# Cross-shaped window attention: where the last stores are issued, how the last sums are grouped, when the second queries are projected, and the order of the work

## The chip, the cores and the metric

The kernel runs on one core of one Trainium2 chip. The metric is the device time of one execution in microseconds. A core has five engines that run side by side, each with its own list of instructions: TensorE (PE, with its weight loads shown apart as PEld), VectorE (DVE), ScalarE (ACT), GpSimd (POOL) and SyncE (SP). They wait for each other only through semaphores. DMAs are issued from the queue of an engine: here SP issues nearly all, ScalarE a few at the beginning and the end.

## The reference

The input x is an image of 224 x 224 positions with 96 channels, in bf16. It is projected to queries, keys and values of 96 channels each. The first 48 channels attend within horizontal stripes of 8 rows, the other 48 within vertical stripes of 8 columns; there are 28 stripes of each kind, and each has 1792 positions. The two halves of the result are put side by side and projected once more.

```python
qkv = jnp.einsum('bhwc,cd->bhwd', x, wqkv)
...
ah = _softmax(jnp.einsum('bqc,bkc->bqk', qh, kh) * scale, axis=-1)
oh = jnp.einsum('bqk,bkc->bqc', ah, vh).reshape(B, H, W, C2)
...
av = _softmax(jnp.einsum('bqc,bkc->bqk', qv, kv) * scale, axis=-1)
ov = jnp.einsum('bqk,bkc->bqc', av, vv).reshape(B, nw, H, sw, C2)
...
return jnp.einsum('bhwc,cd->bhwd', o, wo)
```

## The kernel before, in words

**Pairs, chunks and units.** Two stripes are worked on at once, as a pair P: pairs 0 to 13 are horizontal, 14 to 27 vertical. The 1792 queries of a pair are cut into four chunks (512, 512, 512 and 256, the list CH), the 1792 keys into 14 tiles of 128. A unit is the scores of one key tile (two for the small chunk) against one chunk, for both stripes: 128 x 1024 numbers in two banks of PSUM. TensorE makes them at L1015.

**Two ways to the exponential.** Most units, 1071 of them, go to ScalarE, which takes the exponential from PSUM into a buffer PT (L1037). The others, 301, go to VectorE, which builds the exponential out of integer operations: L1075 turns the scores into integers I_sb, L1088 and L1090 split off two parts (U_sb, E_sb), and L1094 multiplies (G_sb), partly on VectorE and partly on GpSimd in halves of 512. The values are then summed with these weights by TensorE at L968, into one bank a chunk. The 1 that is put beside the values gives the sum of the weights as well.

**What goes on around it.** For each pair the queries (L686, evacuated at L700), keys (L686, L706, centred at L720) and values (L761, L766) are projected while the pair before is worked on. Each finished chunk is copied out of PSUM (L931) and projected with wo: for horizontal pairs at L809, divided by the sum of the weights and kept in Ph_sb (L796, L816); for vertical pairs at L843 (or L847), divided into tmp (L796, L853), added to Ph_sb by GpSimd (L859) and stored (L887).

**The head.** Pair 0 has no pair before it. TensorE makes warm-up matmuls (L532), turns one half of x (L647), projects the keys and the first queries, and two groups of values (L761). Then come the second queries (one matmul at L686, two at L679), then the first scores (L1015). The keys are centred on VectorE in two pieces (L719), the first of 256 columns so that the first scores can start.

**The tail.** In the last pair stores go out in pieces of 16 x 8 x 96, one for each key tile's worth of queries and stripe. Those of the first two chunks, and those of the third chunk's first stripe, are issued by SP (L887); the four of the third chunk's second stripe by ScalarE, behind its last exponential. For the last, small chunk there is no addition on GpSimd: VectorE takes a reciprocal and makes four sums (L866, one a piece of 128 x 96, each a multiply by the reciprocal and an addition of Ph_sb), and four final stores follow (L898), two from SP and two from ScalarE. At the end SP waits until all stores have landed.

**What sets the order.** All instructions are made as records (Op) with the engine, the records they depend on and the buffers that they take. Each engine has several streams of such records: on TensorE 0 is the start-up, 1 and 2 are scores for ScalarE and VectorE, 3 and 4 the value sums of VectorE's and ScalarE's units, 5 output projections, 6 projections of the next pair. Strings of digits in PLAN say, for TensorE, VectorE and GpSimd, from which stream the next instruction comes; "bank" says which PSUM bank each takes and "far" which half products go to GpSimd. The order of each engine is thus written out, and each instruction waits for the semaphores of what it depends on. SP and ScalarE take what is ready by the planner's own reckoning of times.

Of the kernel before, what the change touches and what calls it, by code (L numbers as in the profile page):

```python
# [28 lines left out]
def ndc(P, c):  # L29
# [5 lines left out]
        "00000000000000000066611216162164144116444216331216431241641231431643441163446141541234133164412164412144312314"  # L35
        "31631451431244144126143153121433146124153341143444131235144123414414126413311463643164154134143163124614412614"
        "31145444134124163135164123135412144414412433112344144116344416312351431241641134445312416411463344144121543123"
        "14611364451231441163441233154113444412614412416312513411433444146123153114634413351541241634124136144123144116"
        "34434134124136134125144412316411463441213341146354154164144123133412314412414412316341163444135123164135414124"
        "41441461231634124133113644413312541441231641146344124313411634312441341261441231341441233144114644512316433153"  # L40
        "12416412314313411644431154444416415431531361241544123164114634114453341541231641241634125144144124133114434412"
        "54144113336412461441164431245143126134114533441414612351331241641146343124414411363412531441134464126134125144"
        "12413313412341541441163533416124415312461341144431163444412134412416313361441241541241631146441132331544113444"
        "12641441261331231341145444415412316311463433125144123164114534412341641146334144125413413312416441241641136441"
        "12444133113644312416441215431341241344123144164133123161331146345124153411444412361341134444615415416431313512"
        "44164123164114344412316311453441264134125144144124313312514414414611363354131254144123413416412416411463343141"
        "45124416313412416341241461113443344125144412133316412164412415411433334154124146134126133411634412441544121633"
        "11433544144164123154123146311446341241441164333125144113644512314314412441441612313412361341153444126133411263"
        "41441153444123416411463431333124154124163411264414411534441163354123164145123134412144414613312414312316441231"
        "44146135135312414414412613331163441144464451441331631241534124164114634114433441251344114644126314412514414123"  # L50
        "13412315411344436131641253144124163413514412416411463334143123146124134114644441214461133344125143411442154136"
        "12316412313313414412415441136446133125413124415411364441231544114634413313316441261341241641231441641144334125"
        "41341441231341241541241641146333134415413124414126133123154113644412315441146334154164144412613312316312464144"
        "11644341241334114634124415412415313613412413314364411444412531213314412313414313441241541163344143123154123154"
        "41146346114644611444463134151244415412316412416314412416411333441251344141153344412513341441241341241543164133"
        "14416412316312461441146443123144116336415312415314124413416412416412416412313313415441146341253134123154114464"
        "31244136144115343341431631241631241644126134114644412413311464441231334151244154124164124133113464431152344131"
        "34125134414412313415411463344154164164123163312416313464144126144144123153312414414412315312416411463331344164"
        "31441246144125144313412414414414615312361331231541136444412415411464441133644311344431531241531241641231641146"
        "44412413314441251334141125313341123444136144125144411463331463134125144412416411444334121641163363151244154124"  # L60
        "16312414316412164411433431231541144434415123315441231541144344123416411463341441246144121633113343412416441116"
        "36336124154124153124164134146124133124134134144415412415311633631541264431441254144134114334413441261331446121"
        "63414441231441126413311463441241541241531231614612431431331444144125143123314414412315441115336346113444641541"
        "64146163313613412414412614411344441231534124154124164114644412313412133411464441133633124415412315411344431251"
        "44411433441541241421316311366334166144164123134124144124154123153411466441313412441441231334154124153114444451"
        "312351331144444123313411434412541331241544113444124314311443152334154114421433114431433151534414445"),
    "dve": (
        "00000000000000000333333332332344323232443233313443432323244123443234323321342444133234423233333344133232333414"
        "23334323442322144313233244333233441323323333244312344323232344431323343133332342432344143232332344123443333332"
        "42421234413332344342333232144323323443214442323442424133321333244233344333331333233234431333323234243324124331"  # L70
        "32344323323344133323323444231323443323233244412334333132332443332144323233234431234432323244431333234312332344"
        "33233314423323234432144323423432412443123333244332344333333313323234412333234432321443233133323443232333413342"
        "32324431423443232324443134332312344323323344331323323443231233344234423321234431323234434323344132332323443313"
        "33234423442332124423133334423233443333132332344312333234421233244331332334432332334413232443231234432333234442"
        "41233431323323344323344413332323244314234423233234441344423132323344323344333313232323443214432332333444423144"
        "21244442343233441323323333334431333233234423231442313334234423233441343232334442133333423443232323444123343123"
        "32334443234441333323232344321444323323323214434441323234443233443331333234233442312344232332344344132314234442"
        "33332332334132334344441333233232344321444213323444323233443132332344432133333233244323234441233441332332344432"
        "34413232344432313332332334423324444412332313333323442344413423332444213234432332332334444421214423323333344333"
        "33333132234412332332344421234443132332344323441334232343333343242123323344334424412332313443432334442414423323"  # L80
        "34442144332343424444143333133333"),
    "pool": (
        "00000000022222221212122222222222222222112122222222222222221212122222222222222222221112222222222222222222211122"
        "22222222222222222121212222222222222222221212122222222222222222212112222222222222222222221212122222222222222222"
        "21212122222222222222222221112222222222222222222121212222222222222222222121212222222222222222222212121222222222"
        "22222222212121222222223223222232222121213222233332222322222121212222233322332232222333112122222222233223322331"
        "21213222232222332222121213222222333223222221211322222222333322222213131322223332222322222233321212123223222233"
        "2222222121212332232222223333221311222222332222222222212121232233332232222222222313112233322223333322333333"),
    "far": (
        "11111011110111111101111111111111111011111111110111011111111111111111101111111111111111111111111101111111111111"  # L90
        "11110111111111111111110111111111111111111111111110111011101100111111110010010111111010101101111001110111010111"
        "011110101100110110110111101101110111011100101101111111101011111011010100001000000"),
    "bank": (
        "76547012376502064256045260426402640264026046207420742047024702470240642053053205203520346034604163416416431463"
        "12356135375073057305730460247024602460406240640635046240260426013601376024072407240720420742706420462042604620"
        "43026402640261356035063503603650361356135631573173510357124571351753153153023520375137512642651365135713602460"
# [281 lines left out]
def bass_standalone__window_attn_cswin__vision_kernel(  # L378
# [30 lines left out]
    with es:  # L409
# [780 lines left out]
        def _(e):  # L1190
            emit(e, "sp")
            for b in range(2):
                n = pl.dma_tot.get(id(s_out[b]), 0)
                if n:
                    e.wait_ge(s_out[b], n)
# [28 lines left out]
```

## Time and profile before

| | us |
|---|---|
| median of three runs | 1008.08 |
| the three runs | 1008.08, 1011.19, 1004.94 |
| the profiled execution | 1004.3 |
| its span, first to last instruction | 1002.5 |
| TensorE busy | 988.0 |
| ScalarE busy | 987.6 |
| VectorE busy | 938.5 |
| GpSimd busy | 684.2 |

The profile is of one execution. A line such as L1037 is a line of the kernel before. In a group of instructions "x1071" is their count, and the numbers behind the bar are busy time in us, mean length of one in ns, and idle time of the engine just before them with what ended it. In the timeline the first two columns are start and length in us; instructions of a kind that follow each other are drawn together. "SPq" and "ACTq" are the instructions by which an engine issues a DMA. The granted clock of TensorE is 0.999 of full speed over the execution.

### The profile page before, as it was taken

What the parts mean: (1) busy time and instruction counts of PE and PEld (TensorE: products, weight loads), DVE (VectorE), ACT (ScalarE), POOL (GpSimd) and SP (SyncE); (2) the same over time, 40 slices, a digit from 0 to 9 for tenths busy, and PEclk for the clock granted to TensorE, in tenths of its full rate; (3) what the DMA queues carried; (4) which work ended last, traced back from release to release, by engine and by line L of the source; (5) the groups of instructions that cost most, each with busy time, mean ns of one, the idle gap of its engine ahead of it and who ended that gap; (6) DMA issues with size and microseconds to landing.
All of it is one profiled execution on the core that took longest, in us unless ns stands there. A gap on an engine that the chain in (4) does not pass through costs nothing.

```text
span 1002.5 us, 24560 instructions
## 1 busy us (share of the span) xinstructions
PE 988.0 (99%) x10211; PEld 385.9 (38%) x10211; DVE 938.5 (94%) x1573; ACT 987.6 (99%) x1080; POOL 684.2 (68%) x660
## 2 busy tenths in 40 slices
PE   8999999999999999999999999999999999999997
PEld 3433433343343334334334333433433443343342
DVE  8999999999999999999899999999999999999997
ACT  7999999999999999999999999999999999999997
POOL 3676766667677676777776776776676777677652
PEclk9999999999999999999999999999999999999999
DMA  5102120220112023011111122222122221222012
GB/s 110 39 2 38 38 32 8 38 38 1 39 39 32 8 38 38 2 36 25 27 29 32 25 46 50 54 52 44 34 41 52 53 54 39 52 52 40 13 36 50
DMA packets 164712, 36.92 MB, mean 37 GB/s; under 512 B 164488, under 2 KB 164488, under 8 KB 164600
## 3 DMA queue, kind: packets, MB, share of 16 engines
q1 hardware_dynamic: 163016, 34.80, 18.5%
q8 instruction: 80, 1.31, 0.5%
q10 hardware_dynamic: 1584, 0.55, 0.2%
q14 instruction: 32, 0.26, 0.1%
HBM read 0.44 MB, written 9.63 MB: 10 GB/s over the span
## 4 chain that ended last, share of the span: by engine, by line
ACT 70%; PE 29%; DVE 1%; issue 0%
ACT PT L1037 70%; PE ps L968 13%; PE ps L1015 11%; PE ps L686 2%; PE ps L761 1%; PE ps L843 1%; PE ps L532 0%; PE ps L809 0%; DVE OT_sb L931 0%; PE ps L647 0%; DVE out_sb L866 0%; DVE I_sb L1075 0%; DVE E_sb L1090 0%; DVE U_sb L1088 0%; PE ps L679 0%
## 5 line engine op out<-in xcount | busy, mean ns | idle before, releaser
L1037 ACT ACTIVATE PT<-ps 128x1024 bf16<-128x1024 f32 x1071 | 983.5, 1119 | 2.9 <-PE ps L1015 1.5
L1094 POOL TENSOR_TENSOR G_sb<-I_sb,U_sb 128x512 bf16<-128x512 bf16 x482 | 544.0, 1153 | 250.7 <-DVE E_sb L1090 225.3
L1015 PE MATMUL ps<-QT_sb,KT_sb 48*128 48x512 bf16 (+1 forms) x3136 | 463.0, 356 | 4.7 <-ACT PT L1037 3.0
L1075 DVE TENSOR_SCALAR I_sb<-ps 128x1024 int16<-128x1024 f32 x301 | 367.3, 1220 | 24.6 <-PE ps L1015 21.1
L968 PE MATMUL ps<-PT,V_sb 128*64 128x512 bf16 (+1 forms) x2422 | 363.8, 363 | 1.1 <-ACT PT L1037 1.0
L1015 PEld LDWEIGHTS ps<-QT_sb,KT_sb 48*128 48x128 bf16 x3136 | 123.2, 93 | 307.4 <-ACT PT L1037 223.7
L968 PEld LDWEIGHTS ps<-PT,V_sb 128*64 128x64 bf16 x2422 | 119.2, 109 | 122.5 <-issue 94.9
L968 PE MATMUL ps<-G_sb,V_sb 128*64 128x512 bf16 (+1 forms) x714 | 115.6, 356 | 0.0
L968 PE MATMUL ps<-E_sb,V_sb 128*64 128x512 bf16 (+1 forms) x714 | 109.9, 356 | 0.6 <-DVE OT_sb L931 0.2
L1088 DVE TENSOR_SCALAR U_sb<-I_sb 128x2048 int16<-128x2048 int16 (+1 forms) x161 | 109.2, 678 | 0.2
L859 POOL TENSOR_TENSOR out_sb<-tmp,Ph_sb 128x480 bf16<-128x480 f32 (+1 forms) x84 | 84.9, 1026 | 30.0 <-DVE E_sb L1090 10.7
L1090 DVE TENSOR_SCALAR E_sb<-I_sb 128x2048 int16<-128x2048 int16 (+1 forms) x161 | 104.9, 652 | 0.2 <-PE ps L968 0.2
L686 PE MATMUL ps<-xT_sb,w_sb 96*64 96x512 bf16 (+1 forms) x444 | 77.6, 367 | 0.9 <-ACT PT L1037 0.5
L931 DVE CAST OT_sb<-ps 128x512 bf16<-128x512 f32 x112 | 69.3, 619 | 5.9 <-PE ps L968 5.0
L706 DVE TENSOR_SCALAR_CACHE_REDUCE KT_sb<-ps 128x512 bf16<-128x512 f32 x110 | 67.8, 620 | 7.4 <-PE ps L686 6.8
L700 DVE TENSOR_SCALAR QT_sb<-ps 128x512 bf16<-128x512 f32 (+1 forms) x111 | 68.1, 619 | 5.2 <-PE ps L686 4.1
L766 DVE CAST V_sb<-ps 128x480 bf16<-128x480 f32 (+2 forms) x85 | 51.7, 611 | 3.1 <-PE ps L761 2.8
L968 PEld LDWEIGHTS ps<-G_sb,V_sb 128*64 128x64 bf16 x714 | 36.4, 108 | 47.3 <-issue 28.8
L720 POOL TENSOR_SCALAR KT_sb<-KT_sb,negmean 128x1792 bf16<-128x1792 bf16 x27 | 47.5, 1759 | 10.3 <-DVE E_sb L1090 6.2
L816 DVE TENSOR_TENSOR Ph_sb<-ps,rc 128x480 bf16<-128x480 f32 (+1 forms) x84 | 52.2, 622 | 2.1
L853 DVE TENSOR_TENSOR tmp<-ps,rc 128x480 f32<-128x480 f32 (+1 forms) x84 | 51.9, 618 | 2.2
L968 PEld LDWEIGHTS ps<-E_sb,V_sb 128*64 128x64 bf16 x714 | 33.9, 108 | 43.1 <-issue 21.1
(47 smaller groups left out, 324.4 us busy)
## 6 DMA issues: line engine op xcount, KB each, us to landing
out_dram<-out_sb SPq DMA_DIRECT2D x208, 42.0 KB, 2.1
xT_sb<-in_x_dram SPq DMA_TRANSPOSE x251, 2.4
out_dram<-out_sb SPq DMA_DIRECT2D x22, 24.0 KB, 1.9
Ph_sb<-in_x_dram ACTq DMA_DIRECT2D x1, 336.0 KB, 3.0
out_dram<-out_sb ACTq DMA_DIRECT2D x6, 24.0 KB, 1.9
wo_sb<-in_wo_dram SPq DMA_DIRECT2D x4, 9.0 KB
wo_sb<-one_sb SPq DMA_DIRECT2D x4, 0.0 KB
w_sb<-in_wqkv_dram ACTq DMA_DIRECT2D x1, 54.0 KB, 4.6
```

The lines of the kernel that those rows point to most:

```text
L686: ins = e.matmul(bk[64 * w:64 * w + 64, 0:qs], lhsT=w_sb[0:C, wblk(P, kind), :], rhs=rhs, start=True, stop=True)
L700: return e.tensor_scalar(dst, src, QS, None, ALU.mult)
L706: return e.tensor_scalar(dst, src, 1.0, None, ALU.mult, ALU.add, accum_out=acc)
L859: return e.tensor_tensor(out_sb[b][:, k0:k0 + nk, ws[0], :], t, Ph_sb[:, k0:k0 + nk, j0 + ws[0], :], ALU.add)
L931: return e.tensor_copy(OT_sb[b][:, q0:q0 + qs], bk[:, 0:qs])
L968: return e.matmul(bank(k.bank)[64 * w:64 * w + 64, x0:x1], lhsT=lhs(w, kts[i])[p0:p1], rhs=rhs(w, i, qs)[p0:p1, x0:x1], start=(op.tok["fir ...
L1015: ins = e.matmul(bank(op.tok["s"][w])[:, i * qs:(i + 1) * qs], lhsT=KT_sb[b][64 * w:64 * w + C2, kt * 128:(kt + 1) * 128], rhs=QT_sb[b][64 ...
L1037: a.fn = lambda e: e.activation(PT[a.tok["p"]][:].rearrange("p (s n) -> p s n", s=2), two(q.tok["s"]), ACTF.Exp, scale=LN128)
L1075: return e.tensor_scalar(dst[:, at:at + 1024].rearrange("p (s n) -> p s n", s=2), two(src), 128.0 * ONE, 0.0, ALU.add, ALU.max)
L1088: f.fn = lambda e: e.tensor_scalar(U_sb[y()][:, 0:m], I_sb[y()][:, 0:m], M_FRAC, HALF, ALU.bitwise_and, ALU.bitwise_or)
L1090: x2.fn = lambda e: e.tensor_scalar(E_sb[x2.tok["l"]][:, 0:m], I_sb[y()][:, 0:m], M_EXP, E_LOW, ALU.bitwise_and, ALU.bitwise_or)
L1094: g.fn = lambda e: e.tensor_tensor(G_sb[x2.tok["l"]][:, i0:i1], I_sb[y()][:, i0:i1].bitcast(BF16), U_sb[y()][:, i0:i1].bitcast(BF16), ALU. ...
```

## The change

There are four parts.

1. The four stores of the third chunk's first stripe in the last pair go from SP's queue to GpSimd's, behind the additions there, with a semaphore of their own (s_tail) for which SP waits at the very end.
2. The four last sums become two planned operations of two sums each. Within an operation the two instructions follow without a wait, one signal is given behind both, and then two stores are put out, one from SP and one from ScalarE.
3. The projection of the second queries of pair 0 is held back until the first scores have been issued.
4. All strings of PLAN are new: the order of instructions on TensorE, VectorE and GpSimd, the banks, and the half products that go to GpSimd.

The numbers of units on each engine are as before. The diff without the strings:

```diff
-        s_nat = sem("s_nat")
+        s_nat, s_tail = sem("s_nat"), sem("s_tail")
...
                 if kind == "q":
                     q_ready[(P, c)] = ops[0]
+                    if startup and c == 1:
+                        q_next.append(p)
...
-                    def d4(s, hold=hold, ws=ws, nk=nk, k0=k0):
+                    def d4(h, hold=hold, ws=ws, nk=nk, k0=k0):
                         def f(e, bk, op):
-                            w, k = ws[s // nk], k0 + s % nk
-                            return e.scalar_tensor_tensor(out_sb[b][:, k, w, :], bk[:, s * (C + 1):s * (C + 1) + C], rc[hold[0].tok["r"]][:, s:s + 1],
-                                                          Ph_sb[:, k, j0 + w, :], ALU.mult, ALU.add)
+                            for s in (h, h + 1):
+                                w, k = ws[s // nk], k0 + s % nk
+                                ins = e.scalar_tensor_tensor(out_sb[b][:, k, w, :], bk[:, s * (C + 1):s * (C + 1) + C], rc[hold[0].tok["r"]][:, s:s + 1],
+                                                             Ph_sb[:, k, j0 + w, :], ALU.mult, ALU.add)
+                            return ins
                         return f
...
-                            side = "act" if P == NP - 1 and c == NCH - 2 and ws[0] else "sp"
-                            dm = Op(side, 0.64, 2.0, fn, by + ([act_of[-1]] if side == "act" else []), dma=(s_out[b], 0))
-                            (q_first["act"] if side == "act" else sp_out).append(dm)
+                            side = ("act" if ws[0] else "pool") if P == NP - 1 and c == NCH - 2 else "sp"
+                            dm = Op(side, 1.0 if side == "pool" else 0.64, 2.0, fn, by + ([act_of[-1]] if side == "act" else []), dma=(s_tail if side == "pool" else s_out[b], 0))
+                            (q_first["act"] if side == "act" else pool_o if side == "pool" else sp_out).append(dm)
...
-                            if s == n - 1:
+                            for s in (h, h + 1):
+                                w, k = ws[s // nk], k0 + s % nk
+                                dst = bass.AP(out.tensor, out.offset + (16 * k * W + SW * (j0 + w)) * C, [[W * C, 16], [1, SW * C]])
+                                side = "act" if s % 2 else "sp"
+                                dm = Op(side, 0.64, 2.0, lambda e, dst=dst, k=k, w=w: e.dma_start(dst, out_sb[b][:, k, w, :]), [op], dma=(s_out[b], 0))
+                                (q_first["act"] if side == "act" else sp_out).append(dm)
+                            if h:
                                 rcs.free(hold[0].tok["r"], [op])
...
-                    tail = [("dve", 0.25, d4(i), [], True, dve_ev, [], final(i)) for i in range(n)] if last else [
+                    tail = [("dve", 0.54, d4(i), [], True, dve_ev, [], final(i)) for i in (0, 2)] if last else [
...
             q.kind = "qa"
+            if i == 0:
+                q_next[0].soft = list(q_next[0].soft) + [q]
...
+            n = pl.dma_tot.get(id(s_tail), 0)
+            if n:
+                e.wait_ge(s_tail, n)
```

The numbers in Op are the planner's own costs of an instruction; they steer where SP and ScalarE place an instruction and are no measurements. In the kernel after, the lines below the first change have numbers that are one to eleven higher.

More of the change, by code (lines that the diff above doesn't have):

```diff
@@ new lines @@
+    "pool": (
+        "00000000022222121212222222222222222222121212222222222222222222121122222222222222222221212122222222222222222211"
+        "21222222222222222222221212122222222222222222212121222222222222222221212122222222222222222222121212222222222222"
+        "22222121212222222222222222212121222222222222222222121212222222222222222222221212122222222222222222121212222222"
+        "22222222222221212122222222332222222232233121212222332232233222231311222222223223333322121212222322222222223221"
+        "31313223222232233322222121313222222223333222222121212222333222233222233131212223222232222222221213132222223333"
+        "22332222313112222322223223222233121212222223222233222231313122332222322322222213131322322322223333322332233333"
+        "33"),
```

149 lines of the change are left out of this document (69 added, 80 removed).

## The prediction

> **What bounds the kernel now.** I read the busy shares of the page first, then the chain that ended last, then the waits of ScalarE, the pace of its exponentials stage by stage, and last the two ends of the span.
>
> ```profile
> span 1002.5 us, 24560 instructions
> ...
> PE 988.0 (99%) x10211; PEld 385.9 (38%) x10211; DVE 938.5 (94%) x1573; ACT 987.6 (99%) x1080; POOL 684.2 (68%) x660
> ...
> ACT 70%; PE 29%; DVE 1%; issue 0%
> ...
> L1037 ACT ACTIVATE PT<-ps 128x1024 bf16<-128x1024 f32 x1071 | 983.5, 1119 | 2.9 <-PE ps L1015 1.5
> ```
>
> The reader should see that two engines are named 99% busy, and that the chain puts 70% on ScalarE. One line, the exponential L1037, holds ScalarE for 983.5 of 1002.5 us. TensorE's 99% is softer, as the waits tell:
>
> ```profile
> PEld ps L1015 <- ACT PT L1037: 223.7, 696, 0.8
> ...
> ACT PT L1037 <- PE ps L1015: 1.5, 3, 0.7
> ACT PT L1037 <- PE ps L968: 0.9, 4, 0.3
> ```
>
> TensorE's weight loads for the scores wait 223.7 us for ScalarE to give back banks; ScalarE stands visibly idle for 1.5 + 0.9 = 2.4 us. So the span is three pieces: a head until the first exponential, 1071 exponentials in a row, and a tail behind the last. The middle is paced like this (source view of L1037 in windows; the last two times of a row are the starts of its first and last exponential):
>
> ```profile
> L1037 ACT ACTIVATE PT<-ps x1071: 1018/1116/1300, 9.9 to 994.4; 128x1024 bf16<-128x1024 f32 x179
> ...
> L1037 ACT ACTIVATE PT<-ps x98: 1018/1085/1236, 9.9 to 99.7; 128x1024 bf16<-128x1024 f32 x98
> ...
> L1037 ACT ACTIVATE PT<-ps x111: 1029/1112/1300, 299.0 to 399.8; 128x1024 bf16<-128x1024 f32 x111
> ...
> L1037 ACT ACTIVATE PT<-ps x109: 1018/1109/1257, 699.6 to 799.5; 128x1024 bf16<-128x1024 f32 x109
> ...
> L1037 ACT ACTIVATE PT<-ps x105: 1041/1163/1278, 899.2 to 994.4; 128x1024 bf16<-128x1024 f32 x105
> ```
>
> One exponential lasts 1.1 us but overlaps the next, so the pace is the distance of starts: 984.5/1070 = 0.9201 us in all, 89.8/97 = 0.9258 in the first window, 100.8/110 = 0.9164, 99.9/108 = 0.9250, and 95.2/104 = 0.9154 in the last. The best and the worst window are 1.1% apart: there is waiting in the pace that the idle column, which counts only what the overlap doesn't cover, leaves out.
>
> **Part 1: four stores from SP's queue to GpSimd's, last sums in two operations.** The tail of before, from the timeline:
>
> ```profile
> 993.70 1.78 POOL L859 TENSOR_TENSOR out_sb<-tmp,Ph_sb 128x384 bf16<-128x384 f32 x2 [4.12 <-DVE tmp L853]
> ...
> 994.39 1.21 ACT L1037 ACTIVATE PT<-ps 128x1024 bf16<-128x1024 f32 x1
> ...
> 995.66 0.41 PE L968 MATMUL ps<-PT,V_sb 128*64 128x256 bf16 x4 [0.51 <-ACT PT L1037]
> ...
> 996.11 0.42 DVE L931 CAST OT_sb<-ps 128x256 bf16<-128x256 f32 x1 [1.80 <-PE ps L968]
> ...
> 996.99 0.18 DVE L796 RECIPROCAL rc<-ps 128x4 f32<-128x4 f32 x1 [0.46 <-PE ps L847]
> 997.21 1.38 DVE L866 SCALAR_TENSOR_TENSOR out_sb<-ps,rc,Ph_sb 128x96 bf16<-128x96 f32 x4
> ...
> 989.76 9.67 SPq L887 DMA_DIRECT2D out_dram<-out_sb  x13
> ...
> 995.69 2.80 ACTq L887 DMA_DIRECT2D out_dram<-out_sb  x4
> 998.54 1.26 ACTq L898 DMA_DIRECT2D out_dram<-out_sb  x2
> 999.48 1.26 SPq L898 DMA_DIRECT2D out_dram<-out_sb  x2
> ```
>
> The last sums (L866) are over at 997.21 + 1.38 = 998.59, but SP still works off older stores without a pause: thirteen from 989.76 to 999.43. Its two final stores (L898) go out only at 999.48 and 1000.1. What one costs:
>
> ```profile
> L898 SPq DMA_DIRECT2D out_dram<-out_sb x2: 597/606/615, 999.5 to 1000.1; - x2
> ...
> DMA to landing us min/median/max: 1.9/1.9/1.9
> ...
> SPq L1195 <- DMA out_dram<-out_sb: 1.3, 1, 1.3
> ```
>
> So the last store starts at 1000.1 and lands 1.9 later, at 1002.0; SP waits 1.3 us for it, and the span ends 0.5 later. Four stores fewer leave SP some 4 x 0.65 = 2.6 us earlier, near 996.8, ahead of the first sum: SP then issues when the sums are ready, its last near 998.6, landing at 1000.5. Next in line is ScalarE's queue, which the change leaves as it is: four stores from 995.69, two more at 998.54, the last starting at 998.54 + 0.65 = 999.2 and landing at 1001.1. That is 0.9 us before 1002.0, and I take this as the gain of the tail. If ScalarE's four stores also go at 0.65 (2.6 instead of 2.80 us) it is 1.1.
>
> The four stores on GpSimd stand behind the two additions L859, which end at 993.70 + 1.78 = 995.48; nothing but the end of the program is queued behind them, and SP waits for their own semaphore last of all. The trace of before has no DMA issue on GpSimd, so I bound it. From below: an issue on SP, 0.65 us; the fourth starts at 995.48 + 3 x 0.65 = 997.4 and lands, with 1.9, at 999.3. From above, the longest instruction that GpSimd has at all:
>
> ```profile
> L720 POOL TENSOR_SCALAR KT_sb<-KT_sb,negmean x27: 1758/1758/1761, 31.1 to 948.2; 128x1792 bf16<-128x1792 bf16 x27
> ```
>
> At 1.76 us the fourth starts at 1000.8 and lands at 1002.7. I take 0.9, GpSimd's own smaller step just before (1.78/2): 998.2 and 1000.1, hidden behind ScalarE's 1001.1. The ends make +0.7 of the tail (1002.7 against 1002.0) in place of -0.9.
>
> [...]
>
> The sums in two operations: two instead of four rounds of issue and signal. VectorE operations that don't wait for each other overlap:
>
> ```profile
> 975.09 0.68 DVE L1088 TENSOR_SCALAR U_sb<-I_sb 128x2048 int16<-128x2048 int16 x1
> ...
> 975.69 0.69 DVE L1090 TENSOR_SCALAR E_sb<-I_sb 128x2048 int16<-128x2048 int16 x1
> ```
>
> Starts 0.60 apart at 0.68 long: 0.08 of overlap, against 1.38/4 = 0.345 apart now. Two pairs save at most 2 x 0.12 = 0.24 us, and the first store waits up to 0.3 longer for its pair. Both lie under ScalarE's queue, which is busy until 998.5: cost and gain 0. If that cover went (stores off ScalarE too), the 0.24 would show.
>
> **Part 2: second queries projected behind the first scores.**
>
> ```profile
> 8.88 0.38 PE L686 MATMUL ps<-xT_sb,w_sb 96*64 96x512 bf16 x1
> 8.91 0.60 PE L679 MATMUL ps<-xT_sb,w_sb 96*64 96x256 bf16 x2
> 9.04 0.94 DVE L719 TENSOR_SCALAR KT_sb<-KT_sb,negmean 128x256 bf16<-128x256 bf16 x2
> 9.43 0.11 PEld L1015 LDWEIGHTS ps<-QT_sb,KT_sb 48*128 48x128 bf16 x4 [0.41 <-DVE KT_sb L719]
> ...
> 9.87 13.10 ACT L1037 ACTIVATE PT<-ps 128x1024 bf16<-128x1024 f32 x14 [0.71 <-PE ps L1015]
> 9.90 1.22 DVE L766 CAST V_sb<-ps 128x480 bf16<-128x480 f32 x2
> ...
> 11.03 0.68 DVE L700 TENSOR_SCALAR QT_sb<-ps 128x512 bf16<-128x512 f32 x1
> ...
> 11.63 1.22 DVE L1075 TENSOR_SCALAR I_sb<-ps 128x1024 int16<-128x1024 f32 x1
> ```
>
> Three matmuls leave the place ahead of the first scores. But the scores' weight load at 9.43 waits for the keys on VectorE (L719), not for them; only the end of the projection, 8.91 + 0.60 = 9.51, overhangs 9.43, by 0.08. The gain at the first exponential is between 0 and 0.1; I take 0.1. The moved evacuation (L700, 0.68 us) leaves its place ahead of VectorE's first own exponential, which may start up to 11.63 - 11.12 = 0.5 earlier, behind the value copies. The second queries serve the second chunk, and the first has ten units for ScalarE, some 9 us: the projection has cover. What VectorE gains here is not on the chain (DVE 1%): 0.
>
> **Part 3: the order searched anew.** By the instruction lists the two kernels have the same matmuls and the same 1071 exponentials; two half products move from VectorE to GpSimd. So only the pace can change. Bounds from the windows: 1070 x 0.9154 = 979.5, which is 5.0 less than 984.5; 1070 x 0.9258 = 990.6, 6.1 more. No row says which stalls the new order makes or ends: I take 0, the middle of the two but for 0.5 us, and keep both ends.
>
> **Sum.** -0.9 - 0.1 + 0 = -1.0 us. Against the profiled execution, 1004.3 us (span 1002.5 and 1.8 around it), 1003.3. That execution is the fastest of the four known: 1004.3, 1004.94, 1008.08, 1011.19. The middle of the four is (1004.94 + 1008.08)/2 = 1006.5, and I put the sum there: 1005.5 us, since a median is wanted, and no row explains why others took longer.
>
> **Rivals.** First, the new order is better: all stages at the best window's pace, -5.0, that is 1000.5 us. For it: the spread of windows, and 223.7 us in which TensorE waits and could work ahead. Against it: the visible idle of ScalarE is only 2.4 us.
>
> Second, the other side: the new order is worse. With every bank and buffer bound to an order written out, one late product makes TensorE, and so ScalarE, wait; at the first window's pace everywhere it is +6.1, 1011.6 us. It makes the kernel slower from a pace of 0.9201 + 1.0/1070 = 0.9211 on. For it: half of the quoted windows run slower than that already.
>
> Third, GpSimd's stores land last. It begins at 1.24 us an issue (995.48 + 3 x 1.24 + 1.9 = 1001.1) and eats the tail's whole gain at 1.54. At 1.76, +0.7 - 0.1: 1007.1 us. [...]
>
> Fourth, the tail's stores were not what ended it: then the last landing stays at 1002.0 though SP is idle before, and the time is 1006.5 - 0.1 = 1006.4.
>
> **How the numbers follow.** Forecast (pace within 2 us of before, tail 0.9 shorter) 0.45, with an own range of 1003.3 to 1007.1, the sum on the fastest execution and on the median of the runs; better order 0.25; worse order 0.18; GpSimd last 0.09; tail unchanged 0.03. The range takes in forecast, GpSimd, the unchanged tail and most of the two orders: 1000.5 to 1011.0, which leaves out a third to a half of each order's chance, some 0.18. About 1% is what a measurement of this kernel can tell from no change. Faster than 998.0 needs 2.5 us beyond the best pace: a fifth of the better order, 0.05. Slower than 1018.2 needs 6.6 beyond the worst: a fifth of the worse order, 0.04. Within 1%: 0.91.
>
> **What would show it.** In the profile after, SP's last small stores should end near 997, its final two start near 998 to 999, and the last landing be one of ScalarE's queue, 5.5 to 6 us behind the last exponential's end; a GpSimd issue over 1.24 us, or SP waiting longest for the new semaphore, speaks for the third rival. The first exponential should start 0 to 0.1 earlier, VectorE's first I_sb up to 0.5. The distance from the first to the last exponential, over 1070, is the whole verdict on the order: under 0.918 the first rival, over 0.922 the second. Wrong altogether would be a pace change over 1%, or a tail longer than before.

## The result, and the profile after

| | median us | range us | executions |
|---|---|---|---|
| before | 1006.16 | 1003.33 to 1012.10 | 20 |
| after | 1013.38 | 1008.70 to 1019.46 | 20 |

The ratio is 1.0061 [1.0045, 1.0077] (95% interval): the change makes the kernel 0.6% slower. Single executions of either kernel differ by up to 1.1%, and the longer ones have the lower mean granted clock (after: 1008.70 us at 0.997, 1019.46 at 0.989; before: 1002.92 at 0.998 and 1012.42 at 0.990 among the 23 beside e10); the profile of after (1014.82 us, clock 0.992) is close to its median, that of before (1004.3 us, 0.999) is among the fastest.

The page of after: the span, the chain that ended last by engine, and the exponential's group.

```profile
span 1012.9 us, 24541 instructions
...
ACT 63%; PE 32%; SPq 3%; DVE 1%; issue 1%; DMA 0%; DVEq 0%
...
L1045 ACT ACTIVATE PT<-ps 128x1024 bf16<-128x1024 f32 x1071 | 985.3, 1115 | 12.3 <-PE ps L1021 11.1
```

The exponentials are as long as before (1115 ns against 1119), and there are 1071 of them again. What has grown is the idle time of ScalarE in front of them, from 2.9 to 12.3 us; and SP's queue, which had no share in the chain before, has 3%. The exponentials start between 9.7 and 1005.4 in place of 9.9 and 994.4:

| piece of the span | before | after | difference |
|---|---|---|---|
| head, to the first exponential | 9.87 | 9.67 | -0.20 |
| first to last exponential | 984.53 | 995.71 | +11.18 |
| last exponential's start to the end | 8.10 | 7.56 | -0.54 |
| span | 1002.5 | 1012.9 | +10.4 |

So the tail is shorter, as forecast, and the middle eats it twenty times over. These are two single profiles, 10.4 us apart; the medians are 7.2 apart. The waits of TensorE name the place: here the longest wait of its matmuls in after, then TensorE, ScalarE and SP around it (timeline), and the same stretch in windows. A window's row gives its length, busy time and count for PE, PEld, DVE, ACT and POOL, then the granted clock, the DMA share and GB/s.

```profile
PE ps L687 <- issue: 2.9, 1, 2.9
```

```profile
599.13 11.01 SPq L892 DMA_DIRECT2D out_dram<-out_sb  x16
610.18 18.31 SPq L559 DMA_TRANSPOSE xT_sb<-in_x_dram  x14
628.54 11.42 SPq L892 DMA_DIRECT2D out_dram<-out_sb  x16
```

```profile
L559 SPq DMA_TRANSPOSE xT_sb<-in_x_dram x7: 1240/1241/1926, 640.0 to 648.4; - x7
...
DMA to landing us min/median/max: 2.4/2.5/4.0
```

```profile
647.61 0.41 PE L974 MATMUL ps<-PT,V_sb 128*64 128x256 bf16 x4
650.88 0.41 PE L687 MATMUL ps<-xT_sb,w_sb 96*64 96x512 bf16 x2 [2.86 <-issue]
...
651.62 0.64 PE L974 MATMUL ps<-PT,V_sb 128*64 128x256 bf16 x4
```

```profile
643.01 5.88 ACT L1045 ACTIVATE PT<-ps 128x1024 bf16<-128x1024 f32 x6
651.73 1.02 ACT L1045 ACTIVATE PT<-ps 128x1024 bf16<-128x1024 f32 x1 [2.84 <-PE ps L1021]
653.27 1.94 ACT L1045 ACTIVATE PT<-ps 128x1024 bf16<-128x1024 f32 x2 [0.52 <-PE ps L1021]
656.50 1.02 ACT L1045 ACTIVATE PT<-ps 128x1024 bf16<-128x1024 f32 x1 [1.29 <-PE ps L1021]
```

```profile
650.88:651.40 0.52, 0.52 (x4) 0.21 (x4) 0.07 (x1) 0.00 (x0) 0.52 (x1) 1.00 0.17 41
651.40:661.64 10.24, 10.24 (x55) 3.56 (x55) 5.69 (x12) 6.38 (x7) 3.51 (x4) 0.50 0.23 45
661.64:662.50 0.86, 0.86 (x10) 0.24 (x8) 0.29 (x1) 0.56 (x1) 0.00 (x0) 1.00 0.24 52
```

Read them in order of time. SP puts out 16 stores of an earlier pair from 628.54 to 639.96. Behind them in the same queue stand the last seven transposing loads of pair 19's input (xT_sb); they go out from 640.0 to 648.4 at some 1.3 us each, and the last lands 2.4 us later, near 650.8. TensorE's next instruction is the first projection of pair 19 (L687), which needs all of xT_sb. It starts at 650.88, after 2.86 us of idle time that the view puts down to "issue", having no releaser to name. The order of TensorE is fixed, so everything behind it waits, ScalarE's scores included (2.84 us).

Then comes what I had not priced at all. From 651.40 to 661.64 the granted clock is 0.50: four of TensorE's value matmuls, drawn as 0.41 us before, take 0.64, and ScalarE finds gaps of 0.5, 1.3, 0.4, 1.3 and 0.3 us. Inside these 10.24 us it is busy for 6.38. They follow 2.86 us of idle time, and they are three times 3.41 us, the length of the stretch named next.

A second stretch of half clock lies in the head of after (13.11 to 16.52, 3.41 us), with ScalarE's gaps 0.94 and 0.33 in it. It isn't a mark of the change: of the runs below, four with the old order (e6, e7, e9, e11) and e10 with the new one have such a stretch in the first 20 us of their profiles (mean granted clock 0.83 there, 0.91 in e11 and in after), while those of before, of e1, e3 and e5 with the new order, and of e2, e4 and e8 with the old one have none (1.00). The last section comes back to it.

### The profile page after: what moved, and what is told of

Read it like the earlier page. It is cut to its first block, busy times and chain, and to the rows that moved or that the text cites. A ratio compares the mean times of both kernels' runs of the same rounds, so it can differ in the third digit from the quotient of the medians.

```text
span 1012.9 us, 24541 instructions
## 1 busy us (share of the span) xinstructions
PE 995.3 (98%) x10211; PEld 388.2 (38%) x10211; DVE 939.8 (93%) x1572; ACT 989.4 (98%) x1080; POOL 689.9 (68%) x666
## 4 chain that ended last, share of the span: by engine, by line
ACT 63%; PE 32%; SPq 3%; DVE 1%; issue 1%; DMA 0%; DVEq 0%
ACT PT L1045 63%; PE ps L974 14%; PE ps L1021 13%; PE ps L687 2%; SPq L559 2%; SPq L892 1%; PE ps L764 1%; PE ps L812 1%; PE ps L846 0%; PE ps L533 0%; DVE I_sb L1083 0%; DMA xT_sb<-in_x_dram 0%; DVE KT_sb L707 0%; PE ps L648 0%; DVE out_sb L870 0%
## 5 line engine op out<-in xcount | busy, mean ns | idle before, releaser
L1045 ACT ACTIVATE PT<-ps 128x1024 bf16<-128x1024 f32 x1071 | 985.3, 1115 | 12.3 <-PE ps L1021 11.1
L862 POOL TENSOR_TENSOR out_sb<-tmp,Ph_sb 128x480 bf16<-128x480 f32 (+1 forms) x84 | 85.2, 1026 | 21.0 <-DVE G_sb L1102 11.4
L687 PE MATMUL ps<-xT_sb,w_sb 96*64 96x512 bf16 (+1 forms) x444 | 78.5, 369 | 4.6 <-issue 2.9
```

Of the source, the lines that this page charges most:

```text
L687: ins = e.matmul(bk[64 * w:64 * w + 64, 0:qs], lhsT=w_sb[0:C, wblk(P, kind), :], rhs=rhs, start=True, stop=True)
L862: return e.tensor_tensor(out_sb[b][:, k0:k0 + nk, ws[0], :], t, Ph_sb[:, k0:k0 + nk, j0 + ws[0], :], ALU.add)
L1045: a.fn = lambda e: e.activation(PT[a.tok["p"]][:].rearrange("p (s n) -> p s n", s=2), two(q.tok["s"]), ACTF.Exp, scale=LN128)
```

## The experiments

Two theories. A: the middle is lost in one place, by a load that lands after TensorE asks for it, and by the half clock that follows the idle time. B: the new order is slower throughout, because its strings give TensorE, VectorE and GpSimd a worse pace, and the late load is one sign of many. Of each run the table gives the median, the ratio to before on the same chip with its 95% interval, and the granted clock of the profiled execution; a run has twelve executions, e7 and e9 have six. "Old order" is the kernel before, "new order" the one after.

| run | what it is | median us | ratio | clock |
|---|---|---|---|---|
| after | new order | 1013.38 | 1.0061 [1.0045, 1.0077] | 0.992 |
| e1 | new order, loads before stores | 1009.70 | 1.0025 [1.0008, 1.0042] | 0.998 |
| e2 | old order, loads before stores | 1009.22 | 1.0035 [1.0019, 1.0051] | 0.995 |
| e3 | new order, idle time filled | 1008.60 | 1.0026 [1.0012, 1.0040] | 0.999 |
| e4 | old order, parts 1 and 2 alone | 1005.54 | 0.9983 [0.9962, 1.0003] | 0.999 |
| e5 | new order, two pairs' loads first | 1007.16 | 1.0010 [0.9996, 1.0024] | 0.999 |
| e6 | e4, two pairs' loads first | 1005.76 | 1.0003 [0.9989, 1.0017] | 0.994 |
| e7 | old order, pair 20's load delayed | 1012.57 | 1.0068 [1.0044, 1.0091] | 0.989 |
| e8 | old order, second queries behind the first scores | 1006.54 | 1.0021 [1.0002, 1.0039] | 0.998 |
| e9 | e4, one pair's loads first | 1025.82 | 1.0180 [1.0149, 1.0210] | 0.982 |
| e10 | new order, three pairs' loads first | 1006.59 | 1.0006 [0.9988, 1.0024] | 0.996 |
| e11 | e4 again, more rounds | 1005.71 | 1.0007 [0.9988, 1.0026] | 0.998 |

**e1 and e2: on SP's queue, loads go ahead of stores everywhere.** The two streams of SP change places, in the new order (e1) and in the old (e2).

```diff
-        sp_out, sp_in = (pl.stream("sp", i) for i in range(2))
+        sp_out, sp_in = (pl.stream("sp", 1 - i) for i in range(2))
```

> The changed kernel, with one difference: where a load of x and a store are both ready, SP takes the load first. Theory A (the loss is loads that stand behind blocks of sixteen stores on SP's queue, and the half clock that follows TensorE's idle time of 2.86 us): no wait of TensorE for x at 648 us, no window of 10.24 us at half clock in the middle, mean granted clock about 0.997; time 1005 to 1008 us, 6 to 8 below the changed kernel. Theory B (the new order itself is worse on TensorE, VectorE and GpSimd; the load is only the wait that came last): another wait takes its place, time 1011 to 1014.

> The kernel before with the same difference on SP. Theory A: the loads of before have little to spare too (the least is 1.4 us in the profiled run), and the runs of before near 1011 us are those in which it ran out; so the runs near 1011 go, the median falls by 1 to 3 us to about 1004.5, and the clock is 0.998 or more in each run. Theory B: nothing changes, 1006 with runs at 1011 as before.

In e1 more than half of the loss is gone: 1.0025, and no half clock in its middle; its 1009.70 us lie above the 1005 to 1008 that I had expected. But now the stores are late, and with them the buffers that GpSimd's additions need. The waits of GpSimd in e1 and of TensorE in e2, and e2's windows around the latter:

```profile
POOL out_sb L862 <- DMA out_dram<-out_sb: 11.1, 4, 4.2
```

```profile
PE ps L968 <- POOL G_sb L1094: 2.0, 1, 2.0
```

```profile
785.40:787.80 2.40, 0.38 (x7) 0.11 (x6) 2.24 (x3) 1.39 (x2) 1.21 (x2) 1.00 0.24 47
...
789.20:796.00 6.80, 6.80 (x33) 1.97 (x31) 5.92 (x10) 5.40 (x6) 4.17 (x5) 0.50 0.22 43
```

In before and after GpSimd's additions wait for no store. In the old order the same exchange makes the kernel slower (1.0035): GpSimd is late with a product G_sb, TensorE idles for 2.0 us, and 6.8 us of half clock follow, twice 3.4. By the timelines two of GpSimd's additions start at 781.50 where before has them from 777.9 on; so GpSimd's next product (1.16 us from 783.60 on) falls beside one of VectorE's (from 783.84 on), which takes 1.47 us there against 0.68 in before, where GpSimd runs nothing beside it, and the late G_sb stands behind both. I had expected the old order to gain or to stay, and that was wrong. Loads first throughout moves the late work from one queue to another, and can't decide between A and B by its time. It does show the second half of A in another place: a wait that isn't a load's has the same tail of half clock.

**e3: the wait stays, the idle time is filled.** Twelve matmuls on the warm-up data, into the bank that the projection will take, are put ahead of the wait for pair 19's input; their output is overwritten.

```diff
...
+                    if late and id(sh) in late:
+                        for i in range(NDUM):
+                            eng.matmul(bank(op.tok["b"])[:, :], lhsT=warm[:, 0:128], rhs=warm[:, :], start=True, stop=True)
+                        late = []
                     eng.wait_ge(sh, v)
```

> The changed kernel, and in addition twelve matmuls without use on TensorE just before it waits for the x of pair 19, into the bank that the projection behind them overwrites: TensorE is busy for 2.6 us of its idle 2.86. Theory A with the clock as the larger part: the wait stays about as long, but the window of 10.24 us at half clock at 651 us goes, and with it some 4 to 5 us: 1008 to 1010 us, clock 0.997. If the idle time itself is the loss and not the clock: 1012 to 1014, no gain. Theory B: 1012 to 1014.

TensorE and ScalarE in e3 (timeline), and the window behind:

```profile
645.87 2.76 PE L1179 MATMUL ps<-warm 128*128 128x512 bf16 x12
649.35 0.41 PE L687 MATMUL ps<-xT_sb,w_sb 96*64 96x512 bf16 x2 [0.71 <-DMA xT_sb<-in_x_dram]
```

```profile
643.04 3.77 ACT L1047 ACTIVATE PT<-ps 128x1024 bf16<-128x1024 f32 x4
650.12 14.80 ACT L1047 ACTIVATE PT<-ps 128x1024 bf16<-128x1024 f32 x16 [3.31 <-PE ps L1023]
```

```profile
652.00:662.00 10.00, 10.00 (x80) 3.72 (x78) 9.64 (x18) 10.00 (x13) 4.08 (x4) 1.00 0.25 48
```

The projection waits for its DMA as before, now by name, and ScalarE still loses 3.31 us. But the clock stays at 1.00 and ScalarE is busy for all of the 10 us behind. The median falls from 1013.38 to 1008.60, the ratio from 1.0061 to 1.0026, and the intervals don't meet: more than half of the loss, some 0.35%, is the half clock, and not the wait.

**e5: the late load is taken away.** A third, first stream on SP holds the loads of pairs 18 and 19 alone. Everything else on SP keeps its rule, and the strings of after stay.

```diff
-        sp_out, sp_in = (pl.stream("sp", i) for i in range(2))
+        sp_hot, sp_out, sp_in = (pl.stream("sp", i) for i in range(3))
...
-                load(P + 2, sp_in)
+                load(P + 2, sp_hot if P + 2 in (18, 19) else sp_in)
```

> The changed kernel; only the loads of pairs 18 and 19 go ahead of stores on SP, all others keep the rule that stores go first. Theory A (late load of pair 19, then half clock): the 3.4 us of the wait and the 4.8 of the clock both go: 1004.5 to 1006 us, 1 to 2 us under the kernel before, because the gain of the tail is then left over; the clock is 0.997 or more. Rival C (putting any load ahead of stores delays the additions on GpSimd that wait for free output buffers, as with all loads ahead): 1008 to 1010, as there. Theory B (the new order is worse elsewhere too): 1009 to 1011.

SP and ScalarE in e5 (timeline):

```profile
609.86 21.50 SPq L559 DMA_TRANSPOSE xT_sb<-in_x_dram  x16
631.40 16.39 SPq L892 DMA_DIRECT2D out_dram<-out_sb  x23
```

```profile
639.13 25.34 ACT L1045 ACTIVATE PT<-ps 128x1024 bf16<-128x1024 f32 x27
```

All 16 loads of pair 19 now stand ahead of the stores, and ScalarE runs 27 exponentials without a gap through the stretch where after lost most. The ratio is 1.0010 [0.9996, 1.0024], clear of after's; the median, 1007.16, is above the 1004.5 to 1006 that I had expected. All the rest of the new order is still in it, so what is left for B is some 0.1%, by the interval no more than 0.24%, and in addition what the shorter tail gives back. Its first and last exponentials start at 9.1 and 995.8, 986.7 apart.

**e7: a late load is put into the old order.** Seven useless loads of 16 x 768 values stand on SP ahead of the last two loads of pair 20, which had the smallest reserve in the old order. In before's own trace (the last two loads in the source view, the first projection in the timeline) they start until 677.8 and land 2.4 later, at 680.2, 1.4 us before TensorE comes to them:

```profile
L558 SPq DMA_TRANSPOSE xT_sb<-in_x_dram x2: 1242/1248/1255, 676.5 to 677.8; - x2
...
DMA to landing us min/median/max: 2.4/2.4/2.4
```

```profile
681.58 0.39 PE L686 MATMUL ps<-xT_sb,w_sb 96*64 96x512 bf16 x2
```

```diff
...
+                    if P == 20 and w == 1 and i == 6:
+                        for n in range(7):
+                            fn = lambda e, n=n: e.dma_start(late_sb[:, n, :], bass.AP(x.tensor, x.offset + 16 * n * W * C, [[W * C, 16], [1, SW * C]]))
+                            stream.append(Op("sp", 0.64, 2.0, fn, dma=(s_late, 0)))
...
```

> The kernel before, with seven loads without use (16 x 768 each, some 0.65 us of SP's queue each, 4.5 us together) ahead of the last two loads of pair 20; its margin there was 1.4 us. Theory A: TensorE waits some 3 us for the x of pair 20, and in most runs a window of 10 us at half clock follows: 1011 to 1014 us, clock 0.993 to 0.995. If only the idle time counted: 1009 to 1010 at a clock of 0.998. Theory B, by which a late load is covered by work from elsewhere: 1006 to 1007.

Windows and TensorE's timeline in e7:

```profile
687.84 0.64 PE L691 MATMUL ps<-xT_sb,w_sb 96*64 96x512 bf16 x2 [3.82 <-issue]
```

```profile
687.56:701.20 13.64, 13.36 (x65) 4.03 (x65) 8.74 (x15) 7.14 (x7) 3.39 (x4) 0.50 0.23 46
```

The old order with one late load shows what after shows: 3.82 us of idle time, then 13.64 us of half clock (four times 3.41), of which ScalarE fills 7.14. The ratio, 1.0068 [1.0044, 1.0091], can't be told from that of after; one of the six executions came out at 1006.2, with a clock of 0.998. With e5 this settles it for A as the cause of most of the loss: taking the late load out of the new order takes the loss away, and putting one into the old order makes it.

**e4 and e11: parts 1 and 2 alone.** The old order; at the end of VectorE's string two characters fewer, at the end of GpSimd's four more.

> The kernel before, its own order, with the two parts at the end alone: four stores on GpSimd's queue and the last sums in two operations. The forecast's tail term: 0.9 us shorter behind the last exponential, ratio 0.999. The rival (GpSimd's issues land last): 0.5 to 1 us longer. Neither theory of the loss has a part in it: the runs stay at 1003 to 1012.

> The old order with parts 1 and 2 alone once more, with more rounds, as the candidate that beats both kernels (0.9983, interval 0.9962 to 1.0003). If the gain is the tail's 0.8 us alone, the ratio is 0.9992 and the interval holds 1; if it is what was measured, 0.998 with an interval below 1.

The tail of e4 (timeline):

```profile
995.81 2.28 POOL L891 DMA_DIRECT2D out_dram<-out_sb  x4
...
996.07 2.88 ACTq L891 DMA_DIRECT2D out_dram<-out_sb  x4
...
997.59 1.12 DVE L869 SCALAR_TENSOR_TENSOR out_sb<-ps,rc,Ph_sb 128x96 bf16<-128x96 f32 x4
998.16 1.18 SPq L903 DMA_DIRECT2D out_dram<-out_sb  x2
999.00 1.30 ACTq L903 DMA_DIRECT2D out_dram<-out_sb  x2
```

From the last exponential's start to the end it is 7.33 us, against 8.10 in the profile of before: 0.77 less. But before has the longest tail of the four profiles that have the old one: it is 7.61 in e2, 7.68 in e7 and 7.46 in e8, where SP comes to its two final stores 4.4 to 4.6 us behind the last exponential's start and not 5.1. The two runs, 0.9983 [0.9962, 1.0003] and 1.0007 [0.9988, 1.0026], both hold 1: a gain of 0.08% or less lies under what the executions' spread lets one tell. So this is a candidate that is no slower than before and faster than after, and no version shown to beat both kernels.

**e8: the second queries behind the first scores, alone.** In the old order two characters of TensorE's string change places, and the banks with them. The line of the string:

```diff
-        "00000000000000000066611216162164144116444216331216431241641231431643441163446141541234133164412164412144312314"
+        "00000000000000000066116216162164144116444216331216431241641231431643441163446141541234133164412164412144312314"
```

> The kernel before, with the projection of the second queries behind the first two units' scores and nothing else moved (one place in TensorE's order, the bank digits with it). The forecast's term: the first exponential up to 0.1 us earlier, ratio 0.999 to 1.001. If the half clock at 13 us in the profile of the changed kernel came from this part: 1 to 2 us longer, with a window of 3.4 us at half clock in the head.

From the centring of the keys to the first exponential (timeline of e8):

```profile
8.88 0.94 DVE L719 TENSOR_SCALAR KT_sb<-KT_sb,negmean 128x256 bf16<-128x256 bf16 x2
...
9.65 4.69 ACT L1037 ACTIVATE PT<-ps 128x1024 bf16<-128x1024 f32 x5 [0.62 <-PE ps L1015]
...
11.47 1.22 DVE L1075 TENSOR_SCALAR I_sb<-ps 128x1024 int16<-128x1024 f32 x1
```

The step is 9.65 - 8.88 = 0.77, against 9.87 - 9.04 = 0.83 in before, and 0.82 to 0.83 in e4, e7 and e11. The new heads (after, e5, e10) have 0.77 to 0.78. That is a gain of 0.05 that no time can show. The ratio of 1.0021 just misses 1; since this trace also has a wait of 1.5 us for the load of pair 20 that the profile of before lacks, and e11's has the same wait, I don't put the 0.2% down to the exchange.

**e6, e9 and e10: how much moving a load may cost, and what is left.** e6 is e4 with the loads of pairs 19 and 20 in the first stream, e9 with pair 20's alone, and e10 is after with those of 18, 19 and 23. The line in which e6 and e9 differ:

```diff
-                load(P + 2, sp_hot if P + 2 in (19, 20) else sp_in)
+                load(P + 2, sp_hot if P + 2 in (20,) else sp_in)
```

> The kernel before with the two parts at the end, and with the loads of pairs 19 and 20 ahead of stores; in its profile without the second difference TensorE waited 1.0 us for the x of pair 20. Theory A: that wait goes, 1003.5 to 1005 us, 0.5 to 1.5 under the same kernel without it. Rival C: 1006 or more.

> The old order with the new tail, and only the loads of pair 20 ahead of the stores on SP's queue (the run with pairs 19 and 20 ahead had 1.0003). If the late load of pair 20 is what is left to lose in the old order, TensorE has no idle time over 1 us before the projection of pair 20, the granted clock is 0.998 or more in most runs, and the ratio is 0.997 (the new tail's 0.8 us and some 2 us of the median that the slower runs of the old order add): under 0.9985. If moving loads only makes other work late (stores, and behind them the additions on GpSimd), the ratio is 1.000 to 1.002 and a new wait of over 1 us stands in the trace.

> The new order with the loads of pairs 18, 19 and 23 ahead of the stores (pair 23 had 0.49 us of idle TensorE left, with 18 and 19 alone ahead the ratio was 1.0010). If late loads are the whole loss of the new order, the ratio is 1.000 or less (its shorter tail gives 0.9995) and its fastest run is under 1004.7. If the new order itself is slower too (distance of first to last exponential 986.7 with two loads ahead, against 984.5 in the profile of before: 2.2 us), the ratio stays at 1.001 to 1.002.

SP and TensorE in e9 (timeline), and windows:

```profile
643.55 26.69 SPq L558 DMA_TRANSPOSE xT_sb<-in_x_dram  x20
```

```profile
656.78 0.39 PE L1020 MATMUL ps<-QT_sb,KT_sb 48*128 48x512 bf16 x2
671.61 0.64 PE L686 MATMUL ps<-xT_sb,w_sb 96*64 96x512 bf16 x2 [14.43 <-DMA xT_sb<-in_x_dram]
```

```profile
665.00:671.60 6.60, 0.00 (x0) 0.02 (x1) 0.00 (x0) 0.00 (x0) 0.00 (x0) 0.50 0.22 44
671.60:680.00 8.40, 8.39 (x34) 1.61 (x34) 3.85 (x8) 4.69 (x5) 4.00 (x4) 0.50 0.01 2
680.00:687.00 7.00, 7.00 (x32) 1.64 (x30) 4.46 (x9) 4.41 (x5) 1.73 (x4) 0.50 0.28 57
```

e9 is far off, against my expectation of a gain: 1.018. By SP's list the 20 loads in the first row are one of pair 19, all 16 of pair 20, and only then the last three of pair 19, which TensorE needs first. It waits 14.43 us for them and is at half clock until 687. I had gone by the pair with the least reserve and not by who stood behind it. One late load costs more here than the whole change did: the theory holds, and the repair was wrong. e6, which moves both pairs, keeps their order and stays at 1.0003; its own gain of the tail isn't seen either. Its profile has 0.79 and 0.57 us of waits of TensorE for VectorE near 683, and 3.4 us of half clock behind them. e10 removes the last wait for a load (0.5 us at pair 23) and is at 1.0006 [0.9988, 1.0024], not to be told from e5. Its profile has no wait of TensorE for a load and full clock from 20 to 1000 us. Its fastest executions (1005.2 to 1005.5 at clock 0.999) are still slower than the fastest of before in that comparison (1002.9 to 1003.7), as e5's fastest are (1004.7 against 1003.5): a pace that is 1 to 2 us slower may be left in the new order. That would be B's part; the intervals don't show it.

## Why the prediction was wrong

**The step that failed: "So only the pace can change."** The prediction took part 3 of its sum, the new order, at "0, the middle of the two", between bounds of -5.0 and +6.1 from the best and the worst window of pace in before. These windows show how evenly the work of before runs. They don't show how long before its first use a load lands, and that is what the new strings moved. Pair 19 in before, from the timelines of SP and TensorE:

```profile
630.18 10.92 SPq L887 DMA_DIRECT2D out_dram<-out_sb  x16
641.15 23.91 SPq L558 DMA_TRANSPOSE xT_sb<-in_x_dram  x18
```

```profile
654.61 0.41 PE L686 MATMUL ps<-xT_sb,w_sb 96*64 96x512 bf16 x2
```

By the semaphores that they signal, the first four of the 18 loads are pair 19's. The fourth goes out at 645.4 and, with 2.4, lands near 647.8: 6.8 us before TensorE's projection. In after the last load goes out at 648.4, and TensorE is ready for it at 648.0. Counted in work and not in time, the load is no later: in both traces 691 exponentials have started when it goes out. It is TensorE's new string that asks sooner, behind 691 exponentials in place of 701, and behind 6772 matmuls in place of 6853. SP takes what is ready by the planner's reckoning, so its list changes without a line of the diff, here to seven loads behind the stores in place of four; but its last load of pair 19 keeps its place in the work.

In the profile the middle grew by 11.2 us. That is a pace of 995.7/1070 = 0.9306 us, beyond the 0.922 that the prediction named as the sign of the second rival, and 1.1% slower than before, where a change of over 1% was to mean "wrong altogether". Steps between profiles divide it: 2.2 from before to e5 (984.5 to 986.7), 3.3 from e5 to e3, which has the wait without the half clock (first to last exponential 990.0), and 5.7 from e3 to after, the half clock, the stretch in the head included. Single profiles carry the differences of single executions, so the ratios are the better measure: 0.35% from after to e3, 0.16% from e3 to e5 (whose intervals overlap), 0.10% left.

**The second rival had the mechanism.** "One late product makes TensorE, and so ScalarE, wait" is what happened, with a load in place of a product, at a chance of 0.18. Its price was taken from a pace lost everywhere (+6.1); it was lost at one place, 2.8 us directly and the rest by a half clock of which the profile of before has no row until the exponentials are over (it starts at 1000.45). So the bound of +6.1 bounded nothing, and 1013.4 lies above the range's end, 1011.0. The reserve of each pair's loads could have been read from the trace of before: pair 20 had 1.4 us, and in three other profiles of the same middle (e4, e8, e11) TensorE waits 1.0 to 1.5 us there. This says how little a shift of a load or of its first use may be, while the spread of the pace says nothing of it.

**Part 1 was right in its path and too large in its size.** The tail was to be 0.9 shorter, with ScalarE's queue the last. In e4 SP's two final stores follow the sums at 998.16, as forecast (998 to 999), and ScalarE's last store ends the run. In after SP still works off older stores without a pause until 1009.00, 3.6 us behind the last exponential's start where the forecast had 2.6, and its last store goes out level with ScalarE's (1010.2 and 1010.3). The profiles gain 0.77 (e4) and 0.54 (after) on that of before. But the 8.10 us from which the term was read were one execution's: the four profiles with the old tail have 7.46 to 8.10, 7.71 in the mean, and the nine with the new one 7.32 to 7.79, 7.45 in the mean; in the old order with its own rule on SP it is 7.75 in the mean (before, e7, e8) against 7.33 (e4, e6, e9, e11). So the two parts at the end are worth some 0.3 to 0.4 us, less than half of the term. GpSimd's issues, taken at 0.9 us between bounds of 0.65 and 1.76, are cheaper than all of these (0.53 in the middle):

```profile
L892 POOL DMA_DIRECT2D out_dram<-out_sb x4: 531/534/712, 1006.4 to 1008.2; - x4
...
DMA to landing us min/median/max: 1.8/1.9/2.7
```

So the last of them lands at 1010.9 at the latest, ahead of ScalarE's, which goes out at 1010.3 only, and the third rival is out. None of these issues took more than 0.71 us, though VectorE worked beside them (a copy, a reciprocal and the first of four sums from 1007.17 on). The landing of 1.9 us is that of SP's stores in before. The sums go from 1.38 to 1.12 us, 0.26 for the 0.24 forecast, and stay hidden.

**Part 2 was right in size and wrong in one detail.** The first exponential gains 0.05, within 0 to 0.1. VectorE's first own exponential didn't move ahead: 2.59 us behind the centring's start in before (11.63 - 9.04) and in e8 (11.47 - 8.88), and 2.83 in after. The evacuation of the second queries still stands in front of it.

**"Within 1%" held, at 0.91,** and "slower by over 1%" didn't come about.

## What to carry to other kernels

When an order is made anew, compare the lists of all engines, the DMA queue's too, and read for each load how long before its first use it lands: the load may keep its place and its first use move ahead. A reserve of a microsecond or two can be gone in the next execution: the 1.4 us of pair 20 in before were waits of 1.0 to 1.5 us in e4, e8 and e11. A wait of TensorE is to be priced with the half clock behind it, which here cost more than the wait itself (0.35% against 0.16%); and before a load is moved ahead, look at which load it overtakes.

## What the runs showed of the hardware

**The half clock came in multiples of 3.41 us:** 10.24 after 2.86 us of idle time (after), 13.64 after 3.82 (e7), 6.8 after 2.02 (e2), 3.4 after 0.79 and 0.57 close together (e6), and about 27 in all around e9's 14.43, by the clock of its windows. It didn't begin with the wait, nor at its end: in after TensorE ran at full clock for 0.52 us behind its wait (the first window row of after), and in e7 the clock fell at 687.56, inside the wait that ended at 687.84. In after the changes of the granted clock, at 13.11, 16.52, 651.40, 661.64 and 1009.80, lie whole multiples of 3.41 us apart: 651.40 - 16.52 = 634.88 is 186 times 3.413.

**How much idle time came before it.** Past the head the clock fell with waits of 2.02 us and more (e2, after, e7, e9), and after 0.79 and 0.57, 1.36 together (e6). It stayed at 1.00 after 1.5 (e8, e11), 1.2 and 1.0 (e1) and 1.02 (e4). So at 1.0 to 1.5 us idle time alone doesn't decide, and what else does was not tried.

**The half clock in the head** comes with both orders. The mean granted clock of the first 20 us was 0.91 in after and e11, 0.83 in e6, e7, e9 and e10, and 1.00 in the other seven profiles. What in the head sets it off stays open.

**Issues.** A GpSimd issue of a store of 16 x 8 x 96 took 0.53 us (median), less than the 0.65 that I had put down for SP's. A transposing load took SP some 1.3 us, so that 16 loads and 16 stores, 21.5 us (e5) and 11.4 us (after) in the rows above, fill most of the 35.8 us of a pair (1002.5/28). That leaves SP little room to send a load early.
